# An attention and two-layer MoE kernel: forms kept in SBUF, GpSimd's arithmetic on VectorE, preparation pinned in program order

## The chip, the core and the metric

The program runs on one core of one Trainium2 chip. The metric is device microseconds of one execution; the time of the kernel before is 877.63 us, the median of three runs (875.82 to 878.61). All times below are microseconds unless marked ns.

The engines are called by the names of the profile: PE (TensorE, matmuls), PEld (its weight loads), DVE (VectorE), ACT (ScalarE), POOL (GpSimd), SP (SyncE, which issues the DMAs here).

## What is computed

Attention within chunks of 64 tokens, then two fully connected layers with a hidden size of 2048 each, on 2304 tokens of 512 features. Cut to what matters:

```python
x = attention(q, k, v)             # 4 x 8 heads, 576 tokens in chunks of 64, head size 64
x = x.transpose(...).reshape(2304, 512)

h = x @ w_in                       # layer 1: 512 -> 2048
r = np.maximum(h, 0.0)
x = (s * (r * r) + b) @ w_out      # 2048 -> 512

h = x @ w_in2                      # layer 2: 512 -> 2048
sp = np.log1p(np.exp(h))           # h itself above 20
out = (h * np.tanh(sp)) @ w_out2   # Mish, 2048 -> 512
```

The weight matrices come as 8-byte floats. The kernel loads both halves of each as 32-bit words and puts the 4-byte float together itself: this is the **decode**.

## The kernel before

**Products.** Every fp32 product is made of three matmuls. Each operand is split into a high part of the type float32r (a copy, on ScalarE) and a low part (the operand less its high part, a subtract on VectorE or GpSimd); high by high, low by high and high by low are summed in PSUM.

**Blocks and groups.** The tokens are cut into five blocks of 512, 512, 256, 512 and 512. The 2048 hidden features are 16 chunks of 128 in each layer, taken in groups of four. Groups 0 to 3 belong to layer 1, groups 4 to 7 to layer 2. Group 0 is worked off with the attention in an order written out by hand (START); it is the same in both kernels. Groups 1 to 3 are a loop of 20 steps each (five blocks by four chunks): a step has 12 matmuls into the hidden tile hp (L348, `mm_in`), Relu on ScalarE (L360), square and scale on VectorE (L366), the bias on ScalarE (L371), high part on ScalarE (L375), low part glo on VectorE (L380, all in `ew`), and 12 matmuls of an output two steps older (L400, `do_out`). At a group's last chunk the sum of the four goes from PSUM into the block's ysum on VectorE (L421). In group 3 ysum is x of layer 2; for block 2 it is split at once into high and low (L427, on GpSimd).

**Layer 2.** Blocks 0 and 1, and blocks 3 and 4, are worked as pairs by `pair_phase`: a product of 2 by 2 half blocks with seven multiplications instead of eight. Its right operands are seven **forms** of a pair (b11, t2, b21, t3, t4, t1, b22), which are quarters of the two blocks' x or differences of them; each form is 1 MB with its high and low part. Its left operands are sums of weight tiles (L603, four for each two tiles). There are seven steps, p1, p6, p2, p7, p4, p5, p3, each for u = 0 and 1, so 14 in all, of six matmuls each (L666) into two PSUM tiles hx and two hy. After a step VectorE adds PSUM to a temporary (L696: ur, c, or r), or Mish is taken on ScalarE (L690) with the high part (L691) and the low part on VectorE (L692). Steps p4 and p7 need p1's bank hx free: p7 overwrites what Mish of p2 reads, and p4 adds to the bank that p7's add has read. Between the steps stand the outputs: four old ones after steps 1, 2, 4 and 5 (counted from 0), and the pair's own after 7, 8, 11 and 13. `single_phase` does block 2 in the ordinary way. A group of layer 2 is pair 0, block 2, pair 1.

**Forms before.** `form_steps` makes a form: a subtract on GpSimd (L569; four of the seven need one), the high part on ScalarE (L572), the low part (L573: GpSimd for all of pair 0 and three of pair 1, VectorE for the other four), and a store to DRAM (L575). The forms of pair 0 are made in group 3 from step 11 on, one each step; those of pair 1 in the first pair phase of group 4. Each use, in all four groups of layer 2, reads a form back from DRAM by `stream` (L584). Both live in a ring of five SBUF slots (RING), which are the room of x of layer 1. The order of makings and reads in group 4 is written out by hand (`plan`).

**Decodes.** In groups 3 to 6 the next group's weight tiles are loaded (L143 for w_in, L148 for w_out, both issued by SP) and decoded: L158, two instructions of one input (L165, L168) and two of two inputs (L176, L180), the last four always on VectorE, then the high part on ScalarE (L189, or L616 for sums) and the low part on VectorE (L194, L628, L639). `group_steps` lists these steps of a group, `spread` deals them out evenly over the steps that are left. In groups 4 to 6 dealing begins at step 6 of the first pair phase.

**What sets the order.** The program is written in this order, but a scheduler may move an instruction ahead of others on its engine when the data it needs is there. Each engine then works its queue in that order and waits for semaphores; SP does so with the DMAs.

## Time and profile before

| | before |
|---|---|
| median of three runs | 877.63 us (875.82 to 878.61) |
| the profiled execution | 877.78 us |
| its span in the trace | 876.0 us |
| PE, PEld busy | 852.3, 715.4 us |
| DVE, ACT, POOL busy | 558.4, 404.1, 88.8 us |
| DMA | 126.63 MB, mean 145 GB/s |
| layer 1's last group (group 3) | 366 to 476.3 us |
| layer 2's first pair phase | from 476.3 us |

The profile is of one execution; its own time, 877.78 us, is 1.78 us above the span that the trace covers. An engine's share of busy time is a mean over the whole span, so the 40 slices of the page (21.9 us each) and the tables of single stretches say more: a digit 9 in the row of PE means that it was busy for 90% or more of that slice, and the row PEclk gives the clock that it was granted, in tenths of full speed. In the tables of waits, the engine that waits stands left of the arrow and the one that it waits for on the right.

### The profile page before, as it was taken

Reading aid. Unit: us, or ns where it says so; the run is one execution under the profiler, and the core shown is the slowest. Engines: PE = TensorE matmul, PEld = TensorE weight load, DVE = VectorE, ACT = ScalarE, POOL = GpSimd, SP = SyncE. Lnnn points to the kernel's source line nnn. Section 1 sums busy time; section 2 is a strip of 40 time slices with the busy share of each in tenths; the row PEclk is TensorE's granted clock in tenths of the full one; section 3 lists DMA queues with packets and bytes.
Section 4 is the critical chain, followed back from the end, with each engine's and each line's share of the span. In section 5 each row is a group of like instructions: output and inputs, shape, how many; then the busy total and the mean of one; then the engine's idle time right before and its main releaser. Section 6 shows DMA issues by size and latency. Waiting matters only on the chain.

```text
span 876.0 us, 12215 instructions
## 1 busy us (share of the span) xinstructions
PE 852.3 (97%) x4814; PEld 715.4 (82%) x4814; DVE 558.4 (64%) x948; ACT 404.1 (46%) x703; POOL 88.8 (10%) x63
## 2 busy tenths in 40 slices
PE   8899999999999999999999859999999999999998
...
DVE  4888875269537834598667995365946594444334
...
PEclk9999999999999999999999979999999999999999
...
GB/s 217 270 289 116 85 50 13 51 141 1 1 25 124 45 0 1 73 121 36 67 271 339 152 298 279 230 253 237 145 164 265 264 172 89 199 188 178 129 107 97
DMA packets 90778, 126.63 MB, mean 145 GB/s; under 512 B 58976, under 2 KB 75360, under 8 KB 81760
## 3 DMA queue, kind: packets, MB, share of 16 engines
...
q8 instruction: 38, 0.62, 0.3%
...
## 4 chain that ended last, share of the span: by engine, by line
PE 87%; DVE 6%; DMA 3%; SPq 2%; issue 1%; ACT 1%; DVEq 0%
PE acc L400 42%; PE hp L348 21%; PE hx L666 10%; PE hy L666 8%; SPq L241 2%; DMA wraw<-in_moe_w_in_dram 1%; DVE r L366 1%; PE pa L249 1%; DVE wdec L180 1%; DMA q<-in_k_dram 1%; DVE wdec L176 1%; DMA k<-in_k_dram 1%; DVE ysum L421 1%; PE warm L475 1%; DVE wdec L158 1%
## 5 line engine op out<-in xcount | busy, mean ns | idle before, releaser
L348 PE MATMUL hp<-xhi,w 128*128 128x512 f32 (+1 forms) x640 | 185.1, 371 | 0.0
L400 PE MATMUL acc<-ghi,w 128*128 128x512 f32 (+1 forms) x640 | 163.4, 372 | 0.5 <-DVE ysum L421 0.5
L348 PEld LDWEIGHTS hp<-xhi,w 128*128 128x128 f32 x640 | 115.2, 189 | 20.1 <-issue 0.5
L400 PEld LDWEIGHTS acc<-ghi,w 128*128 128x128 f32 x640 | 112.6, 188 | 20.8 <-ACT r L360 0.9
L348 PE MATMUL hp<-xlo,w 128*128 128x512 f32 (+1 forms) x320 | 117.9, 368 | 0.0
L400 PE MATMUL acc<-w,ghi 128*128 128x512 f32 x352 | 101.8, 399 | 0.7 <-DVE ysum L421 0.7
L400 PE MATMUL acc<-glo,w 128*128 128x512 f32 (+1 forms) x320 | 94.1, 369 | 0.2 <-DVE glo L380 0.2
L380 DVE TENSOR_TENSOR glo<-r,ghi 128x512 fp32r<-128x512 f32 (+1 forms) x73 | 54.5, 747 | 50.3 <-ACT ghi L375 50.1
L421 DVE TENSOR_TENSOR ysum<-acc,ysum 128x512 f32<-128x512 f32 (+1 forms) x114 | 71.5, 655 | 22.4 <-PE acc L400 22.0
L400 PE MATMUL acc<-w,gr 128*128 128x512 f32 x336 | 84.2, 389 | 0.0
L400 PEld LDWEIGHTS acc<-w,ghi 128*128 128x128 f32 x352 | 67.3, 194 | 15.1 <-DVE ysum L421 1.3
L603 POOL TENSOR_TENSOR ws<-wdec 128x256 f32<-128x256 f32 x16 | 20.4, 1292 | 574.7 <-ACT ghi L375 368.4
L360 ACT ACTIVATE r<-hp 128x512 f32<-128x512 f32 (+1 forms) x73 | 40.1, 551 | 79.4 <-PE hp L348 76.4
L696 DVE TENSOR_TENSOR ur<-hy,ur 128x512 f32<-128x512 f32 (+1 forms) x56 | 36.2, 648 | 62.2 <-PE hy L666 51.8
L366 DVE SCALAR_TENSOR_TENSOR r<-r,s_sb 128x512 f32<-128x512 f32 (+1 forms) x60 | 49.8, 830 | 38.3 <-ACT r L360 38.3
L400 PEld LDWEIGHTS acc<-w,gr 128*128 128x128 f32 x336 | 62.7, 188 | 12.7
L348 PEld LDWEIGHTS hp<-xlo,w 128*128 128x128 f32 x320 | 60.2, 188 | 10.2
L400 PEld LDWEIGHTS acc<-glo,w 128*128 128x128 f32 x320 | 58.1, 188 | 11.0 <-DVE glo L380 0.8
L371 ACT ACTIVATE r<-r,b_sb 128x512 f32<-128x512 f32 (+1 forms) x60 | 40.9, 681 | 56.5 <-DVE r L366 56.4
L189 ACT ACTIVATE w<-wdec 128x512 fp32r<-128x512 f32 x56 | 34.9, 628 | 59.7 <-DVE wdec L180 59.6
L400 PE MATMUL acc<-w,glo 128*128 128x512 f32 x176 | 58.5, 393 | 4.0 <-DVE glo L692 4.0
L666 PE MATMUL hy<-xs,wb 128*128 128x512 f32 x192 | 49.0, 390 | 0.1
...
## 6 DMA issues: line engine op xcount, KB each, us to landing
...
xs<-d0t SPq DMA_DIRECT2D x16, 1024.0 KB, 6.4
xs<-d3t SPq DMA_DIRECT2D x16, 1024.0 KB, 5.8
xs<-d0b SPq DMA_DIRECT2D x12, 1024.0 KB, 6.3
xs<-d3b SPq DMA_DIRECT2D x12, 1024.0 KB, 5.3
...
d0t<-xs SPq DMA_DIRECT2D x4, 1024.0 KB, 4.8
```

What stands on the lines that cost most here:

```text
L189: nc.scalar.activation(out=w[:, 0], in_=a, func=AF.Copy)
L241: nc.sync.dma_start(out=t[o:o + n].rearrange("p (h d) -> p h d", h=H), in_=dict(k=k, q=q, v=v)[which][bb, :, ss:ss + n, :].rearrange("h s ...
L348: nc.tensor.matmul(out=hp, lhsT=w[:, sl], rhs=r[b][:, a, :], start=(a == 0 and p == 0), stop=(a == KD - 1 and p == 2),)
L360: nc.scalar.activation(out=r, in_=hp, func=AF.Relu)
L366: nc.vector.scalar_tensor_tensor(out=r, in0=r, scalar=s_sb[:, 0:1], in1=r, op0=ALU.mult, op1=ALU.mult)
L371: nc.scalar.activation(out=r, in_=r, func=AF.Identity, bias=b_sb[:, 0:1])
L380: nc.vector.tensor_tensor(out=lo, in0=r, in1=hi.bitcast(F32), op=ALU.subtract)
L400: nc.tensor.matmul(out=acc[m][:, :n] if l == 1 else acc[m], lhsT=w[wi][:, sl] if l == 1 else g[gi][:, sl], rhs=g[gi] if l == 1 else w[wi], ...
L421: nc.vector.tensor_tensor(out=y, in0=a[:, :w], in1=y, op=ALU.add)
L603: t[o] = lambda o=o, i=i, j=j, op=op: nc.gpsimd.tensor_tensor(out=s[:, o], in0=i, in1=j, op=op)
L666: nc.tensor.matmul(out=out, lhsT=w[i][:, a * P:(a + 1) * P], rhs=x[j][:, a], start=(begins and a == 0 and p == 0), stop=(ends and a == KD ...
L696: nc.vector.tensor_tensor(out=out, in0=i, in1=j, op=ALU.add)
```

## The change

- **GpSimd.** All its tensor arithmetic goes to VectorE: L427, L569, L573 and L603. The two kinds of form tables that chose an engine are gone.
- **Forms.** A list of free slots (`free`) takes the ring's place: four slots, a fifth (xhi3) from step 16 of group 3, a sixth (xlo4) from group 4 on. In group 4 a form is used from the slot it was made in; the slot comes free after its step for u = 1. It is still stored to DRAM, and read back for groups 5 to 7 alone, in the order of `wanted`, whenever a slot is free. The hand-written `plan` is gone: in group 4 the next form is made after each step for which there is a free slot. Scratch for the differences is wx2 and wx3, for both pairs.
- **Pins.** From group 3 on decodes, sums, high and low parts of weights, and the forms' instructions are issued through `quiet`, which holds them in program order on their engine. In the rows below they all have the line L155.
- **Elementwise work of group 3.** With `late`, L366 and L371 give way to a Square and an Identity with scale and bias, both on ScalarE.
- **Order of preparation.** The dealing in group 3 ends four steps earlier; in groups 4 to 6 it begins at step 8, not 6; `group_steps` puts the w_out tiles ahead of the pairs of w_in for groups 5 to 7. The loads of w_out may start one step earlier (i > 5).

```diff
-RING = ("xhi0", "xlo0", "xhi1", "xlo1", "xhi3")
+RING = ("xhi0", "xlo0", "xhi1", "xlo1")
...
+    paced = [False]
+    def quiet(issue, **z):
+        ins = issue(**z)
+        if paced[0]:
+            tc.keep_in_program_order(ins)
...
-            nc.vector.tensor_scalar(
+            quiet(nc.vector.tensor_scalar, 
                 out=a.bitcast(U32), in0=t[:, :, 1], scalar1=0x7FFFFFFF, scalar2=None, op0=ALU.bitwise_and
             )
...
-        if l == 1:
+        if l == 1 and late:
+            nc.scalar.activation(out=r, in_=r, func=AF.Square)
+            nc.scalar.activation(out=r, in_=r, func=AF.Identity, scale=s_sb[:, 0:1], bias=b_sb[:, 0:1])
+        elif l == 1:
             ew_u(r)
             ew_v(r)
...
-    ring = [0]
+    free = list(RING[:4])
     def ring_tile():
-        t = sb.tile([P, 2, 2, TB], F32R, tag=RING[ring[0] % len(RING)], name="xs")
-        ring[0] += 1
-        return t
+        tag = free.pop(0)
+        return tag, sb.tile([P, 2, 2, TB], F32R, tag=tag, name="xs")
...
-                nc.gpsimd.tensor_tensor(out=y[name], in0=i, in1=o, op=ALU.subtract)
-            t = ring_tile()
+                quiet(nc.vector.tensor_tensor, out=y[name], in0=i, in1=o, op=ALU.subtract)
+            tag, t = ring_tile()
             hi, lo = (t[:, z].rearrange("p k n -> p (k n)") for z in range(2))
-            nc.scalar.activation(out=hi, in_=y[name], func=AF.Copy)
-            low[name].tensor_tensor(out=lo, in0=y[name], in1=hi.bitcast(F32), op=ALU.subtract)
+            quiet(nc.scalar.activation, out=hi, in_=y[name], func=AF.Copy)
+            quiet(nc.vector.tensor_tensor, out=lo, in0=y[name], in1=hi.bitcast(F32), op=ALU.subtract)
             stored[pair, name] = d = dram.tile([P, 2, 2, TB], F32R, name=f"d{b0}{name}")
             nc.sync.dma_start(out=d.bitcast(U32), in_=t.bitcast(U32))
+            streamed[NG, pair, name] = tag, t
...
-                t[o] = lambda o=o, i=i, j=j, op=op: nc.gpsimd.tensor_tensor(out=s[:, o], in0=i, in1=j, op=op)
+                t[o] = lambda o=o, i=i, j=j, op=op: quiet(nc.vector.tensor_tensor, out=s[:, o], in0=i, in1=j, op=op)
...
-        r = []
-        for o in range(0, FG, 2):
-            r += pair_steps(f + o) + part_steps(2, f + o, 1) + part_steps(2, f + o + 1, 1)
-        return r
+        pairs = [pair_steps(f + o) for o in range(0, FG, 2)]
+        singles = [part_steps(2, f + o, 1) for o in range(FG)]
+        order = pairs[:1] + singles[:2] + pairs[1:] + singles[2:] if grp == NG else singles[:2] + pairs[:1] + singles[2:] + pairs[1:]
+        return [s for z in order for s in z]
...
-            x = streamed[grp, pair, form]
+            tag, x = streamed[grp, pair, form]
             two_halves(out, wd[fs[u]][w], [x[:, 0], x[:, 1]], begins, True)
+            if u == U[-1]:
+                free.append(tag)
...
-                spread(todo, NB * FG - step)
+                spread(todo, NB * FG - 4 - step)
...
+            if step == 4 * FG:
+                free.append("xhi3")
+            if step > 2 * FG + 2 and free:
                 mix.pop(0)()
...
-        def common():
+        def after(i):
             i = done[0] = done[0] + 1
-            if to_load and (to_load[0][2] == 0 or i > 6):
+            if mix and free and i != 1:
+                mix.pop(0)()
+            while wanted and free and not mix:
+                stream(wanted.pop(0))
+            if to_load and (to_load[0][2] == 0 or i > 5):
                 load_w(*to_load.pop(0))
-            if i == 6 and not final:
+            if i == 8 and not final:
                 todo.extend(group_steps(grp + 1))
             spread(todo, 34 - i)
-        plan = {1: (-1, 3), 3: (-1, 4), 5: (-1, 5), 7: (-1, 6), 9: (-1,), 10: (-1,), 11: (-1,), 13: (7, 8)}
```

Three places show how this moves instructions on the engines. In the rows, names are tiles: wraw a loaded weight tile, wdec its decode, w the tile's high and low part, ur the temporaries, hx and hy the PSUM tiles of the steps, r a temporary of Mish, xs a form's slot, ts scratch, ysum a block's x or sum, d0 the DRAM copies of pair 0's forms; the numbers tell tiles apart.

**VectorE in layer 2's first pair phase.** Before, in its queue between the outputs' sums and the add of the first p7 (the last row):

```order
L421 TENSOR_TENSOR ysum4_2132<-acc3_4532,ysum4_2132 128x512 [waits PE_49]
L168 TENSOR_SCALAR wdec_5047<-wdec_5047 128x512 [waits DVE_49]
L696 TENSOR_TENSOR ur_4591<-hy_4597,ur_4591 128x512 [waits PE_49]
L180 SCALAR_TENSOR_TENSOR wdec_4935<-wraw_4756,wdec_4935 128x512 [waits DVE_49]
L180 SCALAR_TENSOR_TENSOR wdec_4999<-wraw_4658,wdec_4999 128x512 [waits DVE_49]
L176 SCALAR_TENSOR_TENSOR wdec_5047<-wraw_4675,wdec_5047 128x512 [waits DVE_49]
L692 TENSOR_TENSOR glo_4685<-r_4683,ghi_4684 128x512 [waits Activation_49]
L692 TENSOR_TENSOR glo_4697<-r_4695,ghi_4696 128x512 [waits Activation_49]
L194 TENSOR_TENSOR w_4966<-wdec_4935,w_4966 128x512 [waits Activation_49]
L180 SCALAR_TENSOR_TENSOR wdec_5047<-wraw_4675,wdec_5047 128x512 [waits DVE_49]
L639 TENSOR_TENSOR w_5045<-wdec_4999,w_5045 128x512 [waits Activation_49]
L696 TENSOR_TENSOR ur_4591<-hx_4594,ur_4591 128x512 [waits PE_49]
```

After, from the add of the first p7 (the first row) to the decode instructions behind the first p4's add:

```order
L706 TENSOR_TENSOR ur_4573<-hx_4582,ur_4573 128x512 [waits PE_49]
L155 TENSOR_TENSOR xs_4686<-ts_4684,xs_4686 128x1024 [waits DMAHW3_49,Activation_49]
L706 TENSOR_TENSOR ur_4573<-hy_4584,ur_4573 128x512 [waits DVE_49]
L706 TENSOR_TENSOR ur_4573<-hx_4583,ur_4573 128x512 [waits PE_49]
L155 TENSOR_TENSOR ts_4725<-ysum3_2017,ts_4684 128x1024
L706 TENSOR_TENSOR ur_4573<-hy_4585,ur_4573 128x512 [waits DVE_49]
L702 TENSOR_TENSOR gr_4574<-ur_4573,gr_4574 128x512 [waits Activation_49]
L155 TENSOR_TENSOR xs_4727<-ts_4725,xs_4727 128x1024 [waits DMAHW7_49,Activation_49]
L155 TENSOR_SCALAR wdec_4734<-wraw_4691 128x512 [waits DMAHW6_49]
L706 TENSOR_TENSOR r_4744<-hx_4582,ur_4573 128x512 [waits PE_49]
L155 TENSOR_SCALAR wdec_4734<-wdec_4734 128x512 [waits DVE_49] x2
```

Before, three tiles of group 5 were decoded between those adds (wdec_4935, wdec_4999, wdec_5047); after, what stands between p7's adds and p4's is the making of pair 1's forms and the first instructions of one decode. L155 names all pinned instructions.

**SP at the same place.** Before, its queue from the store of the first form on:

```order
L575 DMA d0b11_4213<-xs_4210 128x2048 [waits DMAHW6_49,Pool_49]
L575 DMA d0b21_4370<-xs_4367 128x2048 [waits DMAHW7_49,Pool_49]
L575 DMA d0t3_4259<-xs_4256 128x2048 [waits DMAHW0_49,Pool_49]
L575 DMA d0t2_4317<-xs_4314 128x2048 [waits DMAHW1_49,Pool_49]
L584 DMA xs_4585<-d0b11_4213 128x2048 [waits DMAHW2_49,DMAHW6_49,DMAHW1_49,PE_49]
L584 DMA xs_4587<-d0t2_4317 128x2048 [waits DMAHW7_49,DMAHW3_49,PE_49]
L575 DMA d0b22_4506<-xs_4503 128x2048 [waits DMAHW4_49,Pool_49]
L575 DMA d0t4_4413<-xs_4410 128x2048 [waits DMAHW5_49,Pool_49]
L584 DMA xs_4631<-d0t3_4259 128x2048 [waits DMAHW4_49,DMAHW0_49]
L143 DMA wraw_4605<-in_moe2_w_in_dram 128x4x256 [waits DVE_49,PE_49]
L584 DMA xs_4589<-d0b21_4370 128x2048 [waits DMAHW5_49]
```

After, from the store of the first form on:

```order
L585 DMA d0b11_4231<-xs_4228 128x2048 [waits DMAHW6_49,DVE_49,Activation_49]
L585 DMA d0t3_4279<-xs_4276 128x2048 [waits DMAHW7_49,DVE_49]
L143 DMA wraw_4593<-in_moe2_w_in_dram 128x4x256 [waits DMAHW0_49,PE_49]
L585 DMA d0t2_4339<-xs_4336 128x2048 [waits DMAHW1_49,DVE_49]
L143 DMA wraw_4619<-in_moe2_w_in_dram 128x4x256 [waits DMAHW2_49,PE_49]
L585 DMA d0b21_4386<-xs_4383 128x2048 [waits DMAHW3_49,DVE_49]
L143 DMA wraw_4644<-in_moe2_w_in_dram 128x4x256 [waits DMAHW4_49,PE_49]
L585 DMA d0t4_4464<-xs_4461 128x2048 [waits DMAHW5_49,DVE_49]
L148 DMA wraw_4691<-in_moe2_w_out_dram 128x1024 [waits DMAHW6_49,PE_49]
L143 DMA wraw_4658<-in_moe2_w_in_dram 128x4x256 [waits DMAHW7_49,PE_49]
L148 DMA wraw_4700<-in_moe2_w_out_dram 128x1024 [waits DMAHW0_49,PE_49]
```

The reads of forms (L584) are gone from group 4, and the stores now alternate with weight loads, which wait for PE.

**VectorE in group 5's first pair phase.** Before, from p7's first add to the decodes behind its second:

```order
L696 TENSOR_TENSOR ur_4591<-hx_5347,ur_4591 128x512 [waits PE_49]
L168 TENSOR_SCALAR wdec_5677<-wdec_5677 128x512 [waits DVE_49]
L168 TENSOR_SCALAR wdec_5737<-wdec_5737 128x512 [waits DVE_49]
L176 SCALAR_TENSOR_TENSOR wdec_5615<-wraw_5484,wdec_5615 128x512 [waits DVE_49]
L696 TENSOR_TENSOR ur_4591<-hx_5348,ur_4591 128x512 [waits PE_49]
L176 SCALAR_TENSOR_TENSOR wdec_5677<-wraw_5515,wdec_5677 128x512 [waits DVE_49]
L176 SCALAR_TENSOR_TENSOR wdec_5737<-wraw_5406,wdec_5737 128x512 [waits DVE_49]
L180 SCALAR_TENSOR_TENSOR wdec_5615<-wraw_5484,wdec_5615 128x512 [waits DVE_49]
L180 SCALAR_TENSOR_TENSOR wdec_5677<-wraw_5515,wdec_5677 128x512 [waits DVE_49]
L180 SCALAR_TENSOR_TENSOR wdec_5737<-wraw_5406,wdec_5737 128x512 [waits DVE_49]
L194 TENSOR_TENSOR w_5663<-wdec_5615,w_5663 128x512 [waits Activation_49]
```

After, from p7's two adds to p4's second:

```order
L706 TENSOR_TENSOR ur_4573<-hx_5324,ur_4573 128x512 [waits DVE_49,PE_49]
L706 TENSOR_TENSOR ur_4573<-hx_5325,ur_4573 128x512 [waits DVE_49,PE_49]
L155 TENSOR_SCALAR wdec_5488<-wraw_5450 128x512 [waits DMAHW2_49]
L155 TENSOR_SCALAR wdec_5488<-wdec_5488 128x512 [waits DVE_49] x2
L706 TENSOR_TENSOR r_5498<-hx_5324,ur_4573 128x512 [waits PE_49]
L702 TENSOR_TENSOR glo_5501<-r_5498,ghi_5500 128x512 [waits Activation_49]
L155 SCALAR_TENSOR_TENSOR wdec_5488<-wraw_5450,wdec_5488 128x512 [waits DVE_49] x2
L706 TENSOR_TENSOR r_5529<-hx_5325,ur_4573 128x512 [waits PE_49]
L706 TENSOR_TENSOR ur_4573<-hy_5326,ur_4573 128x512 [waits PE_49]
```

Before, three decodes were worked at once between the adds; after, one decode stands there, in program order, and its first instruction waits for a DMA (DMAHW2_49, the load of wraw_5450, a w_out tile).

## Rows read from the trace of the kernel before

**Rows 1.** The page's parts 1 and 2: busy us by engine; 40 slices, tenths.

```profile
PE 852.3 (97%) x4814; PEld 715.4 (82%) x4814; DVE 558.4 (64%) x948; ACT 404.1 (46%) x703; POOL 88.8 (10%) x63
...
PE   8899999999999999999999859999999999999998
...
DVE  4888875269537834598667995365946594444334
...
PEclk9999999999999999999999979999999999999999
```

**Rows 2.** Windows: stretch, length, busy us (x) by engine, granted clock, DMA, GB/s.

```profile
489.00:526.20 37.20, 24.62 (x91) 18.74 (x91) 37.20 (x47) 14.86 (x22) 22.00 (x10) 0.82 0.58 214
...
366.00:476.30 110.30, 109.59 (x528) 92.19 (x526) 83.37 (x118) 54.21 (x90) 42.20 (x24) 1.00 0.42 155
```

**Rows 3.** Waits of PE: total us, times, longest us.

```profile
PE hx L666 <- DVE r L696: 7.8, 1, 7.8
PE acc L400 <- DVE glo L692: 4.0, 2, 3.0
```

**Rows 4.** Timeline of PE, 425 to 545 us: start us, us, instruction.

```profile
476.30 2.88 PE L666 MATMUL hx<-xs,w 128*128 128x512 f32 x12
479.02 1.98 PE L400 MATMUL acc<-ghi,w 128*128 128x512 f32 x8
...
503.44 3.31 PE L400 MATMUL acc<-w,ghi 128*128 128x512 f32 x8
```

**Rows 5.** Timelines of POOL and DVE around 495 us.

```profile
495.04 2.51 POOL L569 TENSOR_TENSOR tr<-ysum 128x1024 f32<-128x1024 f32 x1 [9.65 <-DVE ysum L421]
497.62 2.71 POOL L569 TENSOR_TENSOR tr<-ysum,tr 128x1024 f32<-128x1024 f32 x1
...
495.81 5.07 DVE L180 SCALAR_TENSOR_TENSOR wdec<-wraw,wdec 128x512 uint32<-128x512 uint32 x2
```

**Rows 6.** Groups of DVE, 481.8 to 526.2 us: busy us, mean ns | idle.

```profile
L180 DVE SCALAR_TENSOR_TENSOR wdec<-wraw,wdec 128x512 uint32<-128x512 uint32 x5 | 7.1, 1437 | 0.0
L176 DVE SCALAR_TENSOR_TENSOR wdec<-wraw,wdec 128x512 uint32<-128x512 uint32 x6 | 6.8, 1130 | 0.0
L573 DVE TENSOR_TENSOR xs<-ysum,xs 128x1024 fp32r<-128x1024 f32 x2 | 6.3, 3148 | 0.0
L628 DVE TENSOR_TENSOR wx<-ws,wx 128x512 fp32r<-128x512 f32 x2 | 2.9, 1474 | 0.0
```

**Rows 7.** Groups of DVE, 570 to 700 us, where GpSimd mostly rests.

```profile
L180 DVE SCALAR_TENSOR_TENSOR wdec<-wraw,wdec 128x512 uint32<-128x512 uint32 x9 | 6.0, 686 | 0.0
L176 DVE SCALAR_TENSOR_TENSOR wdec<-wraw,wdec 128x512 uint32<-128x512 uint32 x9 | 6.0, 685 | 0.0
...
L158 DVE TENSOR_SCALAR wdec<-wraw 128x512 uint32<-128x512 uint32 x12 | 4.8, 424 | 10.3 <-DMA wraw<-in_moe_w_out_dram 6.2 <-DMA wraw<-in_moe_w_in_dram 3.3 <-POOL ws L603 0.7
...
L628 DVE TENSOR_TENSOR wx<-ws,wx 128x512 fp32r<-128x512 f32 x3 | 2.1, 687 | 0.1
```

**Rows 8.** Groups of the whole span, each shape apart.

```profile
L487 ACT ACTIVATE r<-r,b_sb,s_sb 128x512 f32<-128x512 f32 x10 | 8.1, 813 | 0.2
...
L485 ACT ACTIVATE r<-r 128x512 f32<-128x512 f32 x10 | 6.4, 645 | 0.1
...
L572 ACT ACTIVATE xs<-ysum 128x1024 fp32r<-128x1024 f32 x6 | 6.2, 1048 | 0.8 <-DMA d0t<-xs 0.8
...
L573 DVE TENSOR_TENSOR xs<-tr,xs 128x1024 fp32r<-128x1024 f32 x2 | 2.4, 1213 | 0.0
...
L690 ACT ACT_TABLE_LOAD x1 | 1.3, 1283 | 0.0
```

**Rows 9.** Groups of DVE, 366 to 476.3 us (layer 1's last group).

```profile
L366 DVE SCALAR_TENSOR_TENSOR r<-r,s_sb 128x512 f32<-128x512 f32 x17 | 17.3, 1020 | 2.6 <-ACT r L360 2.6
```

**Rows 10.** The page's part 6: DMA issues, KB each, us to landing.

```profile
xs<-d0t SPq DMA_DIRECT2D x16, 1024.0 KB, 6.4
```

**Rows 11.** The w_out loads of L148, all issues.

```profile
DMA to landing us min/median/max: 3.2/4.5/7.4
```

More of the change, by code (lines that the diff above doesn't have):

```diff
@@ L188, in decode_h @@
         wt[l, f, part] = w[:, 0], w[:, 1]
-        nc.scalar.activation(out=w[:, 0], in_=a, func=AF.Copy)
+        quiet(nc.scalar.activation, out=w[:, 0], in_=a, func=AF.Copy)
     def decode_l(l, f, part):
@@ L193, in decode_l @@
         a = raw.pop((l, f, part))[1]
-        nc.vector.tensor_tensor(out=lo, in0=a, in1=hi.bitcast(F32), op=ALU.subtract)
+        quiet(nc.vector.tensor_tensor, out=lo, in0=a, in1=hi.bitcast(F32), op=ALU.subtract)
     def decode_w(*z):
@@ L547, in chunk_attention_moe_moe_kernel, with form_steps @@
     stored = {}
-    ring = [0]
+    free = list(RING[:4])
     def ring_tile():
-        t = sb.tile([P, 2, 2, TB], F32R, tag=RING[ring[0] % len(RING)], name="xs")
-        ring[0] += 1
-        return t
-    def form_steps(pair, scratch, low):
+        tag = free.pop(0)
+        return tag, sb.tile([P, 2, 2, TB], F32R, tag=tag, name="xs")
+    def form_steps(pair, scratch):
         b0, b1 = pair
@@ L615, in high @@
             for to, of in z:
-                nc.scalar.activation(out=to[:, 0], in_=of, func=AF.Copy)
+                quiet(nc.scalar.activation, out=to[:, 0], in_=of, func=AF.Copy)
             a = wt[l, f, 0]
@@ L627, in low @@
             to, of = t["z"][i]
-            nc.vector.tensor_tensor(out=to[:, 1], in0=of, in1=to[:, 0].bitcast(F32), op=ALU.subtract)
+            quiet(nc.vector.tensor_tensor, out=to[:, 1], in0=of, in1=to[:, 0].bitcast(F32), op=ALU.subtract)
         def drop():
@@ L638, in low_a @@
             hi, lo = wt[a]
-            nc.vector.tensor_tensor(out=lo, in0=raw[a][1], in1=hi.bitcast(F32), op=ALU.subtract)
+            quiet(nc.vector.tensor_tensor, out=lo, in0=raw[a][1], in1=hi.bitcast(F32), op=ALU.subtract)
         return [
@@ L696, in add, with copy @@
         nc.vector.tensor_tensor(out=out, in0=i, in1=j, op=ALU.add)
+    def copy(out, i):
+        nc.scalar.copy(out=out, in_=i)
     def out_chunk(grp, b, f, g, o):
@@ L780, in one @@
             two_halves(xb[u], wd[fs[u]]["a11"], x[0], True, True)
-            nc.scalar.copy(out=a[u], in_=xb[u])
+            copy(a[u], xb[u])
         def two(u):
@@ L830, in chunk_attention_moe_moe_kernel @@
             if step >= 4:
[L831 removed]
+                spread(todo, NB * FG - 4 - step)
             if step == 2 * FG + 2:
[L833 to L836 removed]
+                mix = form_steps(PAIRS[0], t_scratch)
+            if step == 4 * FG:
+                free.append("xhi3")
+            if step > 2 * FG + 2 and free:
                 mix.pop(0)()
```

65 lines of the change are left out of this document (22 added, 43 removed).

## The prediction

> **What bounds the kernel now.** I read the page's first two parts, then a table of stretches, the waits, the timelines, and last the groups of VectorE instructions.
>
> TensorE is busy 97% of the span and its digit is 9 nearly everywhere; only the first slices, slices 23 and 24, the last slice and the 8 at the left fall below [rows 1]. So other engines' time counts only where they make TensorE wait. The start is the same in both kernels, and the last 4 us are the final sums and stores. What is left is the stretch in which the second layer begins: from 489.0 to 526.2 us TensorE works 24.62 of 37.20 us while VectorE works all 37.20 [rows 2], and both larger waits of TensorE are on VectorE, 7.8 and 4.0 us [rows 3].
>
> What the stretch costs: idle 37.20 - 24.62 = 12.58 us. Its 91 matmuls are also slow: eight of them take 3.31 us, against twelve that start 2.72 us apart as a block (476.30 to 479.02), 0.227 us each [rows 4], and the granted clock of the stretch is 0.82 [rows 2], so part of it runs at 1.2 instead of 2.4 GHz. Twelve of the 91 have 256 columns; counted as half, the stretch is 85 x 0.227 = 19.3 us of work, so 5.3 us go to the clock. **The stretch loses 12.6 + 5.3 = 17.9 us**, and each idle microsecond costs 17.9 / 12.6 = 1.42. The profiled execution took 877.78 us (span 876.0, 1.78 around it); the median shown, 877.63, is 0.15 lower, so nothing has to be converted.
>
> Why VectorE is full there has two parts. First, GpSimd: two of its subtracts run from 495.04 to 500.3, and two VectorE instructions that start at 495.81 take 5.07 us together [rows 5], where one takes 0.686 undisturbed [rows 7]. In the stretch from 481.8 the four worst groups lose: L180 7.1 - 5 x 0.686 = 3.7, L176 6.8 - 6 x 0.686 = 2.7, L628 2.9 - 2 x 0.687 = 1.5, L573 6.3 - 2 x 1.213 = 3.9 us [rows 6 to 8], together 11.8 us of 44.4. Second, work that nobody needs yet: the 16 decode instructions of L158, L165, L168, L176 and L180 that stand among the first adds of the layer are group 5's, 90 us early. The order of before shows them between the adds, three weight tiles at once.
>
> **GpSimd's arithmetic to VectorE.** Per pair of weight tiles four sums of 256 columns (32 in all), 8 subtracts and 10 low parts of 1024, four low parts of the single block. A 1024-wide one costs VectorE 1.213 us [rows 8], a narrow one at most 0.687 [rows 7]. The 18 wide ones make 21.8 us, the 36 others at most 24.7, over some 390 us; GpSimd's 88.8 us of work [rows 1] go, and with them its collisions. Where that lands decides, so I go by stage.
>
> **Group 3 (366 to 476 us).** VectorE is busy 83.37 of 110.30 us, TensorE 109.59 [rows 2]. Added: 5 wide low parts and 3 or 4 wide subtracts, 9 x 1.213 = 10.9; 8 sums and 4 narrow low parts, at most 12 x 0.687 = 8.2. Removed: L366, which goes to ScalarE as a Square and a scaled Identity; its 17 wide ones alone are 17.3 us [rows 9]. So VectorE stays near 85 of 110 us. ScalarE gets at most 20 x (0.645 + 0.813) = 29.2 us on top of 54.21 [rows 2, 8], still under 110. The tightest place is steps 12 to 17, where decode and forms meet: the order has some 30 us of VectorE work there for 30 us of matmuls. Each step's glo is wanted only two steps later (8 to 11 us), and steps 18 and 19 bring almost no work, so a lag of up to about 6 us is caught up. Cost: nothing; without that cover, the lag times 1.42.
>
> **The first pair phase (from 476.3).** At full clock: 14 blocks of 6 matmuls, two outputs of layer 1 and four of layer 2, 156 x 0.227 = 35.4 us. In the order of after, VectorE has in these rows 11 wide instructions (13.3 us), 20 of 512 columns (13.7 us) and the first decode (five instructions, 3 x 0.424 + 2 x 0.686 = 2.6 us [rows 7]): 29.6 of 35.4 us, 84%, and the adds that TensorE waits for no longer stand behind three decodes. I followed the two chains by hand, with T = 0 at the first matmul. Released slot: the sixth block (t2's last reader) ends at T = 10.9; ScalarE's hi of the next form (1.05) and the table load (1.28) come first [rows 8], then Mish of p2, done at T = 13.8; TensorE reaches p7, which needs that bank, at 16.3. Slack 2.5 us. VectorE's add for p7 ends at T = 18.4 and p4 wants it at 22.9. Slack 4.5 us. The later ones have more. So all 12.6 us of idle go, and with them the low clock. What is late next is that first Mish; I leave 1.1 us for it and its like.
>
> **Forms kept in SBUF.** The 14 reads of 1 MB in group 4 go (6.4 us to landing [rows 10]); TensorE's waits on them go from the order too. Six slots instead of five hold a form from making until its last block; then the slot is refilled, six forms ahead, some 16 us of matmuls at least, against 6.4. The stores stay. They now stand behind weight loads that wait for TensorE (SP's order), but each has landed 10 us or more before its slot is written again. Cost and gain: nothing on the path, as TensorE never waited for a form [rows 3].
>
> **Pinned decodes, w_out first, earlier end in group 3.** The pin holds an instruction behind what was written before it on its engine; others may still pass. It moves the group 5 decodes out of the stretch into the rest of group 4. It adds one wait: in groups 5 and 6 the first decode waits for a w_out load and VectorE's queue stands behind it. The load is issued when the third old output ends; 7.7 us of matmuls later VectorE gets to the decode, and TensorE needs the add behind it 8 us after that. Landing takes 3.2 to 7.4 us [rows 11]. Cost nothing, up to a landing of about 16 us.
>
> **Sum:** 877.78 - 17.9 + 1.1 = 861.0 us.
>
> **The port, by rows and by page.** The rows show a VectorE instruction with two SBUF inputs ending when GpSimd's does [rows 5]. The Trainium skill, SBUF — State Buffer, Who interferes with whom, says that the later one blocks for the whole of the other's instruction. By it VectorE could have lost up to GpSimd's 22.00 us in this stretch [rows 2], not the 11.8 counted here; the sum stays, since it goes by TensorE's loss, but the gain would be surer.
>
> **Rivals.**
> *B, part stays.* The 2.5 us of slack at the first Mish is eaten, because ScalarE's pinned hi waits for TensorE's release, or VectorE lags out of group 3. For: ScalarE and VectorE each have these releases in one queue. Against: the slacks above. With half the idle left, 6.3 x 1.42 = 9 us: 869.
>
> *C, VectorE stays the bound.* If the decodes stayed where they are, VectorE would need 44.4 - 11.8 + GpSimd's six wide ones (7.3) and eight narrow ones (at most 5.5) = 45 us for the stretch, as now: 877. The order speaks against it. The Trainium skill, Perfetto Trace Analysis, Optimizing Scalar/DVE Operations, says that a saturated VectorE may be helped by giving work to ScalarE or even GpSimd, with the warning that the port is shared; taken alone it speaks against this change and for C. No run here shows which half weighs more.
>
> *D, slower.* The head of VectorE's queue waits for w_out in groups 5 and 6. For 880.3 us it would take (880.3 - 859.9) / 1.42 = 14.4 us of idle, 7.2 in each group, so a landing 23 us after issue; at 24 us the time is 882. Against it: the 7.4 us above. From 16 us on it costs something.
>
> *E.* That the change does not do what it says: GpSimd has no arithmetic left in the order, so this is out.
>
> **How the numbers follow.** Chances: A (the sum, 861) 0.62, B (869) 0.19, C (877) 0.10, D (882) 0.09. About 0.3%, 2.6 us, is what a measurement of this kernel can tell from no change. Faster takes A and B, 0.81; same C, 0.10; slower D, 0.09. Low end: all 17.9 us, the 0.7 us that TensorE idles in group 3 (110.30 - 109.59), and 1.8 us of spread of the runs: 857.4. High end: B with two thirds of the idle left, 859.9 + 8.4 x 1.42 = 872. A and most of B lie in it.
>
> **What would show it.** Right: the matmul digit 9 through slices 22 to 24 and the granted clock 1.00 there; no TensorE wait on VectorE over 2 us; VectorE near 85% in the first pair phase and its 512-wide instructions at 0.69 us throughout; the first decode of group 5 after p4's adds; no GpSimd row; group 3 still without idle. Wrong: TensorE waiting for ScalarE's Mish near the start of the layer (B), for glo in steps 14 to 19 (B out of group 3), for an add of p4 in groups 5 and 6 with a decode waiting on a DMA ahead of it (D).

## The result

The kernel after takes 856.94 us (median of 4 runs, 855.81 to 857.34), the kernel before 877.48 us beside it (875.82 to 878.61). The ratio is 0.9765 with a 95% interval of 0.9747 to 0.9784: 2.35% faster. The prediction was 861.0 us with a range of 857.4 to 872.0. Direction and mechanism were right; the gain was 20.5 us where 16.6 were forecast, and the time lies 0.46 us below the range.

The page of after, parts 1 and 2, answers to [rows 1]:

```profile
PE 846.2 (99%) x4814; PEld 712.9 (83%) x4814; DVE 550.6 (64%) x982; ACT 415.9 (49%) x723; POOL 3.4 (0%) x9
...
PE   8999999999999999999999999999999999999998
...
DVE  4888985249735943333798598845886398835244
...
PEclk9999999999999999999999999999999999999999
```

TensorE has no slice under 9 between the first and the last, its clock was granted in full in every slice, and GpSimd is left with 3.4 us. The waits of TensorE that the trace of after lists (total us, times, longest) all belong to the attention at the start, these two ahead; those of [rows 3] are gone:

```profile
PE pt__100 L257 <- DMA k<-in_k_dram: 4.0, 1, 4.0
PE pt__399 L257 <- DMA k<-in_k_dram: 0.7, 1, 0.7
```

**Where the time went.** I cut both traces at the same places of the program: the first matmul of group 3's block 2, the start of layer 2, and the third step of block 2 in group 4. Windows of before (stretch, length, busy us of PE, PEld, DVE, ACT, POOL, granted clock, DMA share, GB/s):

```profile
419.94:476.30 56.36, 55.65 (x290) 47.51 (x288) 37.29 (x40) 26.36 (x46) 29.46 (x15) 1.00 0.60 227
476.30:542.66 66.36, 53.78 (x230) 43.01 (x228) 59.30 (x82) 28.41 (x46) 26.45 (x15) 0.90 0.70 261
```

Windows of after, the same two stretches, then the first pair phase and the whole of group 3 from 366 us on, which answer to [rows 2]:

```profile
419.23:474.37 55.14, 55.14 (x289) 47.54 (x288) 44.38 (x79) 38.29 (x66) 0.00 (x0) 1.00 0.37 131
474.37:522.42 48.05, 48.05 (x230) 40.45 (x229) 41.38 (x62) 24.87 (x39) 0.00 (x0) 1.00 0.56 223
...
474.37:510.00 35.63, 35.63 (x164) 29.73 (x163) 28.99 (x38) 19.49 (x28) 0.00 (x0) 1.00 0.56 219
366.00:474.37 108.37, 108.37 (x524) 91.61 (x523) 66.18 (x117) 64.86 (x107) 0.00 (x0) 1.00 0.28 96
```

From the start of layer 2 to the last cut the gain is 66.36 - 48.05 = 18.31 us: 12.58 us of idle time (66.36 - 53.78) and 53.78 - 48.05 = 5.73 us by which the same 230 matmuls were slower before. The end of group 3 gave 56.36 - 55.14 = 1.22 us, of which 0.71 was idle; the other 0.51 lies in the matmuls' own times and was not followed further. The start gave 0.71 us; in both kernels the first matmul of 256 columns marks its end, and from there to the first cut both take 316.60 us. Before:

```profile
103.34 0.39 PE L348 MATMUL hp<-xhi,w 128*128 128x256 f32 x2
```

After:

```profile
102.63 0.39 PE L356 MATMUL hp<-xhi,w 128*128 128x256 f32 x2
```

After the last cut the gain is 0.20 us, the time outside the span included (333.34 + 1.78 against 333.18 + 1.74). Together 18.31 + 1.22 + 0.71 + 0.20 = 20.44 us, the difference of the two profiled executions (877.78 and 857.34).

**The two chains followed by hand.** ScalarE of after, the table load and the first Mish of p2 (start us, us, instruction):

```profile
486.53 1.28 ACT L700 ACT_TABLE_LOAD   x1
487.82 0.60 ACT L700 ACTIVATE r<-hx 128x512 f32<-128x512 f32 x1
```

TensorE of after: p2 for u = 0 and 1, the first p7, the first p4:

```profile
485.25 2.88 PE L676 MATMUL hx<-xs,w 128*128 128x512 f32 x12
...
490.69 1.52 PE L676 MATMUL hx<-xs,wx 128*128 128x512 f32 x6
...
497.27 1.52 PE L676 MATMUL hx<-xs,wx 128*128 128x512 f32 x6
```

VectorE of after: the first p7's add, the first instruction of the first decode, and the first p4's add:

```profile
492.25 0.69 DVE L706 TENSOR_TENSOR ur<-hx,ur 128x512 f32<-128x512 f32 x1 [0.15 <-PE hx L676]
...
499.10 0.42 DVE L155 TENSOR_SCALAR wdec<-wraw 128x512 uint32<-128x512 uint32 x1
499.44 0.69 DVE L706 TENSOR_TENSOR r<-hx,ur 128x512 f32<-128x512 f32 x1
```

With T = 0 at 474.37 us the prediction had Mish done at 13.8 (488.17 us; measured 487.82 + 0.60 = 488.42), TensorE at p7 at 16.3 (490.67; 490.69), p7's add done at 18.4 (492.77; 492.94) and p4 at 22.9 (497.27; 497.27). Both slacks held, 2.3 and 4.3 us, so nothing of the 1.1 us set aside was needed. VectorE was busy 28.99 of 35.63 us, 81% where 84% was forecast. One sign came out a little otherwise: the first decode begins 0.34 us ahead of p4's first add, not behind it, and nothing waits for it.

### The profile page after: what moved, and what is told of

Same layout as the page of the kernel before. It is cut to its first block, busy times and chain, and to the rows that moved or that the text cites. A ratio compares the mean times of both kernels' runs of the same rounds, so it can differ in the third digit from the quotient of the medians.

```text
span 855.6 us, 12134 instructions
## 1 busy us (share of the span) xinstructions
PE 846.2 (99%) x4814; PEld 712.9 (83%) x4814; DVE 550.6 (64%) x982; ACT 415.9 (49%) x723; POOL 3.4 (0%) x9
## 4 chain that ended last, share of the span: by engine, by line
PE 97%; DMA 1%; ACT 1%; SPq 0%; DVE 0%; issue 0%; DVEq 0%
PE acc L411 46%; PE hp L356 23%; PE hx L676 12%; PE hy L676 9%; PE warm L486 1%; PE pa L257 1%; DMA wraw<-in_moe_w_in_dram 1%; PE pa L283 1%; ACT pbd L319 0%; DMA k<-in_k_dram 0%; SPq L249 0%; PE pa L328 0%; DVE ysum L432 0%; PE pt__567 L328 0%; PE pt__100 L257 0%
## 5 line engine op out<-in xcount | busy, mean ns | idle before, releaser
L411 PE MATMUL acc<-w,ghi 128*128 128x512 f32 x352 | 98.7, 390 | 0.0
L388 DVE TENSOR_TENSOR glo<-r,ghi 128x512 fp32r<-128x512 f32 (+1 forms) x73 | 46.2, 633 | 68.4 <-ACT ghi L383 68.4
L155 DVE SCALAR_TENSOR_TENSOR wdec<-wraw,wdec 128x512 uint32<-128x512 uint32 x128 | 87.0, 688 | 1.7
L411 PEld LDWEIGHTS acc<-w,ghi 128*128 128x128 f32 x352 | 65.4, 188 | 13.1
L155 DVE TENSOR_SCALAR wdec<-wdec 128x512 uint32<-128x512 uint32 (+1 forms) x128 | 53.1, 423 | 5.7 <-ACT wdec L155 4.1
L374 DVE SCALAR_TENSOR_TENSOR r<-r,s_sb 128x512 f32<-128x512 f32 (+1 forms) x40 | 27.9, 696 | 36.4 <-ACT r L368 36.4
L155 ACT ACTIVATE w<-wdec 128x512 fp32r<-128x512 f32 x56 | 35.0, 627 | 32.1 <-DVE wdec L155 32.0
```

The lines of the kernel that those rows point to most:

```text
L155: ins = issue(**z)
L374: nc.vector.scalar_tensor_tensor(out=r, in0=r, scalar=s_sb[:, 0:1], in1=r, op0=ALU.mult, op1=ALU.mult)
L388: nc.vector.tensor_tensor(out=lo, in0=r, in1=hi.bitcast(F32), op=ALU.subtract)
L411: nc.tensor.matmul(out=acc[m][:, :n] if l == 1 else acc[m], lhsT=w[wi][:, sl] if l == 1 else g[gi][:, sl], rhs=g[gi] if l == 1 else w[wi], ...
```

## The experiments

The main theory: VectorE's queue ahead of p4's adds held more work than TensorE's matmuls there, partly by collisions with GpSimd, partly by decodes that were put there. The rivals make one or the other of them the whole cause. Medians, with before beside each between 876.3 and 877.5 us:

| kernel | us | ratio to before, 95% |
|---|---|---|
| after | 856.94 | 0.9747 to 0.9784 |
| 1 before + pins | 879.48 | 1.0016 to 1.0042 |
| 2 before + VectorE for GpSimd | 865.93 | 0.9860 to 0.9889 |
| 3 after, no pins | 859.71 | 0.9791 to 0.9820 |
| 4 after, GpSimd's work back | 865.09 | 0.9842 to 0.9887 |
| 5 after, forms re-read | 869.03 | 0.9889 to 0.9923 |
| 6 after, square on VectorE | 857.66 | 0.9757 to 0.9801 |
| 7 after, Mish 12 copies late | 865.04 | 0.9842 to 0.9874 |
| 8 after, forms on GpSimd | 866.25 | 0.9845 to 0.9899 |
| 9 forms re-read, no pins | 864.74 | 0.9842 to 0.9874 |
| 10 after, Mish 8 copies late | 860.33 | 0.9793 to 0.9826 |
| 11 after, sums on GpSimd | 857.18 | 0.9763 to 0.9792 |
| 12 forms re-read, their instructions unpinned | 856.86 | 0.9758 to 0.9790 |

### 1. Pins alone

```diff
 # before, with quiet() and paced as in after, GpSimd's instructions too
-            nc.scalar.activation(out=hi, in_=y[name], func=AF.Copy)
-            low[name].tensor_tensor(out=lo, ...)
+            quiet(nc.scalar.activation, out=hi, in_=y[name], func=AF.Copy)
+            quiet(low[name].tensor_tensor, out=lo, ...)
```

> The kernel before with one part of the change: the decodes, pair sums, high and low parts of weights and the forms' instructions pinned in program order from group 3 on; GpSimd keeps its arithmetic, forms are re-read, loads and dealing as before. Theory 1 (two causes: VectorE's queue between the first p6's add and the second p4's add holds more work than the about 21 us of matmuls there, partly hoisted decodes, partly collisions with GpSimd): the queue holds 13.7 us of undisturbed work here against 24.4 before, so even with collisions of up to 12 us it just about fits; time 857 to 863. Rival 2 (collisions with GpSimd are the whole cause): little moves, 873 to 878. Rival 3 (hoisted decodes are the whole cause): 856 to 859.

Measured 879.48 us, a little slower than before. All three ranges missed: theory 1 by 16 us, the nearest, rival 2, by 1.5. The stall moved. TensorE's timeline (in brackets the idle time ahead, and who ended it):

```profile
473.07 1.19 PE L408 MATMUL acc<-ghi,w 128*128 128x512 f32 x2 [4.16 <-DVE ysum L429]
...
492.74 0.73 PE L408 MATMUL acc<-ghi,w 128*128 128x512 f32 x2 [2.66 <-ACT ghi L383]
...
510.67 4.83 PE L674 MATMUL hx<-xs,wx 128*128 128x512 f32 x13 [2.50 <-DMA xs<-d0t]
```

The first row stands in group 3, the second at layer 1's last outputs, which are worked off in layer 2's first pair phase; neither is at p4. The third waits for a form's read. Beside the second, VectorE (two small decode instructions):

```profile
484.00 5.16 DVE L155 TENSOR_SCALAR wdec<-wdec 128x512 f32<-128x512 f32 x2
```

and GpSimd at that time:

```profile
483.76 2.57 POOL L155 TENSOR_TENSOR xs<-ts,xs 128x1024 fp32r<-128x1024 f32 x1 [1.17 <-ACT xs L155]
486.29 2.58 POOL L155 TENSOR_TENSOR xs<-ysum,xs 128x1024 fp32r<-128x1024 f32 x1
```

Two instructions of 0.42 us took 5.16, ending just after GpSimd's (488.87). Behind them in VectorE's queue stands the square and scale (L374, at 490.52 us) of the output whose ghi TensorE waits for. So pins by themselves don't help while GpSimd's wide instructions run beside the decodes around the end of group 3. How much of the loss comes from the pinned forms and how much from the pinned decodes wasn't separated.

### 2. VectorE alone

```diff
-                nc.gpsimd.tensor_tensor(out=y[name], in0=i, in1=o, op=ALU.subtract)
+                nc.vector.tensor_tensor(out=y[name], in0=i, in1=o, op=ALU.subtract)
 # and so for L427, L573 and L603; nothing else
```

> The kernel before with one part of the change: all GpSimd arithmetic on VectorE, nothing pinned, forms re-read. Theory 1: no collisions, but the queue between the first p6's add and the second p4's add now holds 27.4 us of work with decodes hoisted as before, some 6 us too much; with 1.42 us lost for each idle one this is about 9 us above the time of after: 864 to 871. Rival 2 (collisions are all): 856 to 859. Rival 3 (hoisted decodes are all): 874 to 880. The tight steps 12 to 17 of group 3 also take L366 here; if they lag, TensorE waits for glo there, 2 to 6 us more.

Measured 865.93 us, as theory 1 said: 11.4 of the 20.5 us. What is left is the wait of [rows 3] at the same place, 5.6 us in place of 7.8:

```profile
PE hx L666 <- DVE r L696: 5.6, 1, 5.6
```

### 3. After without pins

```diff
-        paced[0] = grp == NG - 1
+        paced[0] = False
```

> The kernel after without the pins; all else as in after. Theory 1: 26.1 us of VectorE work stand between the first p6's add and the second p4's add, some 5 us too much, 7 us lost: 861 to 867. Rival 2 (collisions are all): 856 to 858. Rival 3 (hoisted decodes are all): 870 to 877.

Measured 859.71 us, 2.8 above after and 1.3 under theory 1's range: the queue alone said too much. Neither rival fits. TensorE waits twice for an add on hy:

```profile
PE hy L676 <- DVE ur L706: 1.4, 2, 1.2
```

### 4, 8 and 11. GpSimd's work back, in parts

```diff
 # 4: all, and block 2's low parts; 8: the forms' two lines alone; 11: the sums' line alone
-                quiet(nc.vector.tensor_tensor, out=y[name], in0=i, in1=o, op=ALU.subtract)
+                quiet(nc.gpsimd.tensor_tensor, out=y[name], in0=i, in1=o, op=ALU.subtract)
...
-            quiet(nc.vector.tensor_tensor, out=lo, in0=y[name], ...)
+            quiet((nc.vector if pair == PAIRS[1] and name in ("t3", "b21", "t1", "b22") else nc.gpsimd).tensor_tensor, out=lo, in0=y[name], ...)
...
-                t[o] = lambda o=o, i=i, j=j, op=op: quiet(nc.vector.tensor_tensor, out=s[:, o], ...)
+                t[o] = lambda o=o, i=i, j=j, op=op: quiet(nc.gpsimd.tensor_tensor, out=s[:, o], ...)
```

> The kernel after with GpSimd's arithmetic back where it was (pair sums, form subtracts, low parts of pair 0 and of three forms of pair 1, block 2's low parts), pinned. Theory 1: VectorE's own work between the first p6's add and the second p4's add is 14.8 us, plus up to 12 us of collisions; near the 21 us there: 857 to 863. Rival 2 (collisions are all): 870 to 877, with VectorE instructions of 2 us and more in that stretch and TensorE waits on them. Rival 3 (hoisted decodes are all): 856 to 858.

> The kernel after with only the forms' work back on GpSimd (eight subtracts, ten low parts of 1024 columns, 2.4 to 2.9 us each); pair sums and block 2's low parts stay on VectorE. With all of GpSimd's work back the time was 865.1, with one VectorE instruction at 2.5 to 2.9 us beside nearly every wide GpSimd instruction that started while VectorE was busy. Theory 4 (each GpSimd instruction holds the VectorE instruction beside it for as long as it runs itself, so wide ones do the harm): 862 to 865, VectorE instructions of over 2 us next to the wide ones only. Rival (the pins tie VectorE's queue to GpSimd's pair sums, which are in the order ahead of decodes): 857 to 860.

> The kernel after with only the pair sums back on GpSimd (32 of 256 columns, about 1 us each), pinned. Theory 4 (a GpSimd instruction holds one VectorE instruction for its own length): four sums fall into group 3's full steps, 3 to 4 us of VectorE time, caught up before the layer's end; the others fall where VectorE has room: 857 to 859. Rival (pins across the two engines make VectorE's decodes wait for the sums and drain its queue): 861 to 866, with TensorE waits on glo or on adds and no long VectorE instruction beside them.

Measured 865.09, 866.25 and 857.18 us. The first is above theory 1's range and under rival 2's; the second just above theory 4's; the third fits theory 4. So the wide instructions of the forms do all the harm that can be measured, 8 to 9 us, and the pair sums none, though each still takes GpSimd about 0.9 us (kernel 11, groups of POOL: busy us, mean ns):

```profile
L155 POOL TENSOR_TENSOR ws<-wdec 128x256 f32<-128x256 f32 x16 | 14.6, 913 | 704.2 <-ACT r L394 409.0 <-DVE wdec L155 276.5 <-ACT w L155 18.7
```

Kernel 4 shows one thing more: with GpSimd's work still in place the rest of the change gains 12.2 us (877.28 to 865.09). The move to VectorE gains 11.4 alone (kernel 2); the two together gain 20.5, so they overlap.

In kernel 8 TensorE's larger waits are in group 3:

```profile
PE acc L411 <- DVE ysum L432: 2.6, 1, 2.6
PE acc L411 <- DVE glo L388: 2.0, 2, 1.6
```

Its GpSimd:

```profile
463.15 2.85 POOL L155 TENSOR_TENSOR xs<-ysum,xs 128x1024 fp32r<-128x1024 f32 x1
465.95 2.84 POOL L155 TENSOR_TENSOR ts<-ysum,ts 128x1024 f32<-128x1024 f32 x1
...
502.86 2.99 POOL L155 TENSOR_TENSOR xs<-ts,xs 128x1024 fp32r<-128x1024 f32 x1 [1.56 <-ACT xs L155]
505.81 2.58 POOL L155 TENSOR_TENSOR ts<-ysum,ts 128x1024 f32<-128x1024 f32 x1
```

and its VectorE at the same times:

```profile
463.67 5.68 DVE L155 SCALAR_TENSOR_TENSOR wdec<-wraw,wdec 128x512 uint32<-128x512 uint32 x2
...
504.10 0.67 DVE L706 TENSOR_TENSOR ur<-hx,ur 128x512 f32<-128x512 f32 x1
504.70 1.44 DVE L155 TENSOR_SCALAR wdec<-wraw 128x512 uint32<-128x512 uint32 x1
506.05 0.68 DVE L706 TENSOR_TENSOR ur<-hy,ur 128x512 f32<-128x512 f32 x1
506.65 2.48 DVE L155 TENSOR_SCALAR wdec<-wdec 128x512 f32<-128x512 f32 x2
```

At 463.67 us two decode instructions with both inputs in SBUF, 0.69 us each elsewhere, take 5.68 and end just after GpSimd's second (465.95 + 2.84 = 468.79): each was held for about as long as one GpSimd instruction ran. The rows from 504.10 us on show who isn't held: the adds that read one input from PSUM (hx, hy) take 0.67 and 0.68 us while GpSimd runs; the decodes with one SBUF input take 1.44 and 2.48 (two) in place of 0.42 each, until GpSimd's end (505.85 and 508.39).

### 5, 9 and 12. Forms re-read

```diff
 # 5: before's ring, plan and stream() in all of layer 2, and its scratch; all else as in after
-            streamed[NG, pair, name] = tag, t
...
+        plan = {1: (-1, 3), 3: (-1, 4), 5: (-1, 5), 7: (-1, 6), 9: (-1,), 10: (-1,), 11: (-1,), 13: (7, 8)}
...
 # 9: as 5, and
-        paced[0] = grp == NG - 1
+        paced[0] = False
...
 # 12: as 5, and
-            quiet(nc.scalar.activation, out=hi, in_=y[name], func=AF.Copy)
-            quiet(nc.vector.tensor_tensor, out=lo, in0=y[name], ...)
+            nc.scalar.activation(out=hi, in_=y[name], func=AF.Copy)
+            nc.vector.tensor_tensor(out=lo, in0=y[name], ...)
```

> The kernel after without one part: group 4's forms are again read back from DRAM through the ring of five slots in the old hand-written order of makings and reads; GpSimd without arithmetic, pins, late elementwise work and order of preparation as in after. Prediction on record (forms kept in SBUF give nothing on the path): 856 to 858. Rival (in a full SP queue the reads come late and TensorE waits for a form, as it did for 2.5 us in the kernel with pins alone and 0.4 us in the one with VectorE alone): 858.5 to 863, with TensorE waits on the reads in the first pair phase.

> The kernel after without two parts: forms re-read in group 4 as before, and nothing pinned. With pins the re-read cost 12 us: b21's read was issued at 482.5 us behind weight loads that wait for TensorE, and landed 10.5 us later. Without pins the stores and reads stand ahead of those loads in SP's queue, and b21 is made early. Theory 5 (the price of reading back is the pinned order, in which b21 is stored late and its read stands behind loads): 859 to 863, near the kernel without pins that keeps its forms (859.7), TensorE waits on form reads under 1 us. Rival (reading 1 MB back while stores and loads fill the DMA engines costs time by itself): 866 to 872, with TensorE waits on the reads of several us.

> The kernel with re-read forms and pins (869.0), but the forms' own instructions not pinned; decodes, sums, high and low parts of weights stay pinned. In the pinned one b21's form was read back at 482.5 us, after its slot's last store and behind two weight loads that wait for TensorE, and landed 10.5 us later. Here b21 and b22 come second and fifth among the stores, and b21's read stands ahead of all but one of the weight loads. Theory 5 (the 12 us are the order in which forms are made and SP's queue behind it): 857 to 862, TensorE waits on form reads under 1 us. Rival (reading back costs by itself, through the DMA engines, which are full at that time): 866 to 870, TensorE waits on a form read of several us. Between them, 862 to 866, if form making ahead of time fills VectorE's queue ahead of p4's adds, with TensorE waits on an add.

Kernel 5 took 869.03 us: 12 us more than after, and above the ranges of both. TensorE waits once for b21:

```profile
PE hx L677 <- DMA xs<-d0b: 8.3, 1, 8.3
```

Its SP queue, the last weight loads and then that read:

```profile
479.34 3.05 SPq L148 DMA_DIRECT2D wraw<-in_moe_w_out_dram  x2
482.49 0.46 SPq L595 DMA_DIRECT2D xs<-d0b  x1
```

and what the DMA engines did meanwhile (window as above; the last two columns):

```profile
484.00:493.00 9.00, 0.75 (x4) 0.29 (x2) 4.37 (x5) 3.29 (x3) 0.00 (x0) 0.77 1.02 424
```

The read is issued at 482.49 us, behind loads that wait for TensorE, and lands at about 493, with the DMA engines full meanwhile (a share of 1.02, 424 GB/s). That looked like a price of reading back. Kernel 9 shows that it isn't: without pins no read is late, and the time is still 864.74, which missed theory 5's range, since now TensorE waits for VectorE:

```profile
PE hx L677 <- DVE r L707: 4.7, 1, 4.7
```

```profile
500.48 1.21 DVE L155 TENSOR_TENSOR xs<-ysum,xs 128x1024 fp32r<-128x1024 f32 x1
...
501.95 1.22 DVE L155 TENSOR_TENSOR xs<-tr,xs 128x1024 fp32r<-128x1024 f32 x1
503.08 1.22 DVE L155 TENSOR_TENSOR tr<-ysum,tr 128x1024 f32<-128x1024 f32 x1
...
506.09 1.28 DVE L707 TENSOR_TENSOR r<-hx,ur 128x512 f32<-128x512 f32 x2
```

Unpinned form, decode and sum instructions, three of them 1024 columns wide, stand between 500.48 and 506.09 us ahead of p4's adds (the last row). Kernel 12 settles it. Pinned weights and unpinned forms give 856.86 us, the time of after, with every form read back and no wait of TensorE on one; b21's read is issued here at 458.39 us, 24 us earlier:

```profile
458.39 1.47 SPq L595 DMA_DIRECT2D xs<-d0b  x1
```

So reading back costs nothing when forms may be made early and decodes may not. Pinning the forms makes b21 late, and there the SBUF copy saves it. The copy has a worth without pins too: kernel 3, with it, took 859.71 us, kernel 9, without it, 864.74.

### 6. Square and scale on VectorE

```diff
-ew(l, hp, sizes[b], grp == NG - 1)
+ew(l, hp, sizes[b], False)
```

> The kernel after without one part: in group 3 the square and scale go back to VectorE, the bias to ScalarE. VectorE has 18.75 of 20 us of work at 439 to 459 us in after; some four of the moved instructions of 0.7 us fall there, 21.5 us, a lag of 2 us against the about 6 that the prediction says are caught up. Theory 1 (a lag under 6 us costs nothing): 856.5 to 858.5, VectorE near 80 of 108 us in group 3. Rival (the lag comes out of group 3 as waits on glo or ysum, with the clock's share): 860 to 866.

Measured 857.66 us, theory 1; no wait of TensorE in group 3. The tight 20 us of after:

```profile
439.00:459.00 20.00, 20.00 (x96) 16.78 (x95) 18.75 (x35) 16.68 (x28) 0.00 (x0) 1.00 0.35 130
```

and of this kernel:

```profile
439.00:459.00 20.00, 20.00 (x96) 16.78 (x95) 19.95 (x38) 13.15 (x23) 0.00 (x0) 1.00 0.22 79
```

VectorE is full there for 20 us without TensorE losing any.

### 7 and 10. A late Mish

```diff
             step(2, xb[u], "a12", "b21", False, u)
+            if first and pair == PAIRS[0] and u == 0:
+                for _ in range(12):    # 10: range(8)
+                    quiet(nc.scalar.activation, out=xb[u], in_=xb[u], func=AF.Copy)
             g[0, u] = mish(xb[u], TB)
```

> The kernel after with twelve extra copies of hx onto itself on ScalarE ahead of group 4's first Mish of p2 (values unchanged), 12 x 0.59 = 7.1 us. In after that Mish ends at 488.42 us and TensorE reaches p7 at 490.69: 2.3 us of slack. So TensorE waits about 4.8 us once. Theory 1 (each idle microsecond costs 1.42 with the clock's share): 6.8 us more than after, 863 to 865. Rival (idle time costs itself alone here; the low clock needs the longer or repeated stalls of before): 861 to 862, granted clock 1.00 in the stretch. Rival (the delay is absorbed): 857 to 858.

> As the run with the late Mish, with eight copies in place of twelve, 8 x 0.6 = 4.8 us; that run gave 5.25 us of idle for 7.2 us of copies, so 1.95 us of slack, and 8.1 us of time. TensorE waits 2.85 us once. Theory 1 (the clock's share comes with the idle time, a factor of 1.4 to 1.55): 860.9 to 861.4. Rival (a wait this short leaves the clock alone): 859.5 to 860.1, granted clock 1.00.

Measured 865.04 us, the upper end of theory 1, and 860.33 us, between the two ranges; there the trace decides. With twelve copies, ScalarE and the first p7 on TensorE:

```profile
487.08 7.33 ACT L155 ACTIVATE hx<-hx 128x512 f32<-128x512 f32 x12 [0.30 <-PE hx L676]
```

```profile
496.37 5.40 PE L676 MATMUL hx<-xs,wx 128*128 128x512 f32 x12 [5.25 <-ACT r L700]
```

With eight:

```profile
485.67 4.88 ACT L155 ACTIVATE hx<-hx 128x512 f32<-128x512 f32 x8 [0.30 <-PE hx L676]
```

```profile
492.51 4.61 PE L676 MATMUL hx<-xs,wx 128*128 128x512 f32 x12 [2.79 <-ACT r L700]
```

The slack is 7.33 - 5.25 = 2.08 us and 4.88 - 2.79 = 2.09 us; the prediction had 2.5. The twelve matmuls behind the wait take 5.40 and 4.61 us in place of 2.88 (0.45 us each in the first, half the pace, the level of 1.2 GHz), so the clock adds 2.52 and 1.73 us: an idle microsecond costs 7.77 / 5.25 = 1.48 and 4.52 / 2.79 = 1.62, where the prediction had 1.42. After's profiled 857.34 us and these sums give 865.11 and 861.86 us; the profiled executions took 865.52 and 860.91. Kernel 10's start was 1.14 us shorter than after's, which covers its difference of 0.95:

```profile
101.49 0.39 PE L356 MATMUL hp<-xhi,w 128*128 128x256 f32 x2
```

Kernel 10's granted clock after its wait of 2.79 us (window as above; the third column from the end):

```profile
492.00:498.00 6.00, 5.49 (x17) 4.36 (x18) 3.88 (x6) 3.04 (x5) 0.00 (x0) 0.72 0.00 0
```

The rival of kernel 10 had it at 1.00 and falls.

## Why the prediction was right or wrong

- **What bounds the kernel: right.** All but 2.1 of the 20.44 us came from the stretch it named (cut here from 476.30 to 542.66 us), and the idle time and the low clock went together.
- **The stretch's 17.9 us: a little small.** 18.31 us. Idle time was exact (12.58); the clock's share came out as 5.73 us against 5.3. The 91 matmul records counted there are a part of those cut here.
- **The step that failed: the small terms beside the stretch.** The sum gave 1.1 us back for a late Mish and put everything outside the stretch at nothing. Measured: the Mish cost nothing, since its slack held, and outside the stretch lay 2.13 us: 1.22 in group 3 (the 0.71 of idle was known and put into the low end alone), 0.71 at the start, 0.20 at the end. With 1.1 + 0.41 + 2.13 = 3.64 us the forecast of 861.0 becomes the profiled 857.34; the median is 0.40 lower still. The start is luck: it is the same program, but its end lies between 101.49 and 103.34 us in the executions traced, and before's is the longest of them.
- **The low end: too tight.** It took off 17.9 and 0.7 us and 1.8 for the spread of the runs. But 0.41 + 0.51 + 0.71 + 0.20 = 1.83 us that the sum had not counted used up the 1.8, and nothing was left for the spread: the median came out 0.46 under it. A margin taken off the likeliest time when every chain has slack belongs into the range alone.
- **GpSimd's work on VectorE: right, about half of the gain**, 11.4 us alone (kernel 2) and 8.2 with the rest in place (kernel 4). VectorE did not get busier by it: 558.4 us over the span before, 557.2 in kernel 2. In group 3 it fell from 83.37 to 66.18 us, where "near 85" was forecast: the collisions in the 83.37 were not taken out (a glo of 512 columns took 0.97 us there before, 0.69 after), and the narrow instructions cost about 0.42 us, not 0.687.
- **The page on SBUF**: the Trainium skill, SBUF — State Buffer, Who interferes with whom, says that whoever comes later blocks for the whole of the other's instruction, and that a VectorE instruction with at most one SBUF input outside the modes with two ports is free of it. Kernel 8 agrees: 5.68 us for two instructions beside 2.85 + 2.84 of GpSimd, and 0.67 and 0.68 us for adds with one input from PSUM. Its decodes with a single SBUF input were held (1.44 us in place of 0.42); by the rule they would be in such a mode, which no row names. The 22 us that the prediction worked out from the rule as a bound could not be told from its 11.8, since TensorE's loss set the sum.
- **Rivals.** B's and D's waits did not come: no wait on Mish, and the longest landing of a w_out load was 7.1 us. C fell with the order it rested on; its half of the truth is in kernels 2 and 9, which leave the decodes unpinned and read forms back, 9.0 and 7.8 us above after. With forms in SBUF (kernel 3) unpinned preparation costs 2.8.
- **Pins: half right.** With GpSimd's work gone they are worth 2.8 us (kernel 3 to after) or, on the weights alone with forms read back, 7.9 (kernel 9 to 12); by themselves they make the kernel slower by 0.3% (kernel 1). What they are worth inside kernel 4 was not tried. "Others may still pass" missed that pinned forms are made late.
- **Forms kept in SBUF, "cost and gain nothing": right by kernel 12, and misleading by kernel 5.** The argument was that TensorE never waited for a form before. That was so because forms were made early there. In the changed order the copy in SBUF is what makes the pinned forms harmless, and without pins it is worth 5.0 us together with its order of makings (kernel 9 to 3).

In steps that were run, from before: GpSimd's work to VectorE 877.3 to 865.9; late elementwise work and the new order of preparation to 864.7 (kernel 9; 1.2 us, near the spread of these runs); pinned weights to 856.9 (kernel 12). Forms in SBUF with pinned forms end at the same 856.9. The order of preparation was not tried apart.
